# A recurrent attention layer fused with a maxout network: a new hand-written order of all engines and loads, grouped by matmul tile shape

## The chip, the cores and the metric

The kernel runs on one core of a Trainium2 chip. Time is device microseconds (us) of that core. PE is TensorE, the matrix engine; PEld is its weight load, which overlaps with matmuls; DVE is VectorE, ACT ScalarE, POOL GpSimd, and SP the engine that mostly issues DMAs. Each engine works through its own list of instructions in order and waits on semaphores for the others.

## What is computed

```python
def _attn_ref(q, k, v, alpha):                 # (4, 8, 768, 48) each
    state = np.zeros((B, H, D, D))
    for t in range(S):
        state = alpha[:, :, t, :, None] * state + np.einsum('bhd,bhe->bhde', k[:, :, t], v[:, :, t])
        y[:, :, t] = np.einsum('bhd,bhde->bhe', q[:, :, t], state)

def _moe_ref(x, w1, w2, w3, w_out):            # x: the y of all heads, (3072, 384); w1..w3 (384, 768)
    h = np.maximum(np.maximum(x @ w1, x @ w2), x @ w3)
    return h @ w_out
```

The state of each of 4 x 8 heads is a 48 x 48 matrix that decays by alpha and takes up one outer product per token; the 8 heads of a token, side by side, are the input of the maxout network.

## The kernel before

The 768 tokens of a batch are cut into chunks of 256 (W), so there are 12 steps: step s is chunk s // 4 of batch s % 4. Within a chunk two blocks (U) of 128 tokens are kept apart, and each partition holds a pair (R) of neighbouring tokens. A step loads alpha, q, k and v (384 KB each) into rings of four buffers, and computes the recurrence in its chunked form: sums of log alpha over the block by a matmul with a triangular matrix (`sums`, lines 234 to 242), exponentials of these sums (line 246), q and k scaled by them (line 266), scores of q against k (line 310), a mask (lines 316 and 320), then the product of masked scores and values together with the product of q and the state carried in (line 331), and the state's update (lines 389, 401, 405, 412). The first five steps turn q and k by TensorE transposes (line 289) and a copy; the later ones by transposing DMAs (line 296).

The network follows: `gate` (line 453) multiplies x by w2 - w1 and w3 - w1, `maxed` (lines 462 to 466) takes maxima with zero, and `project` (line 487) multiplies the result by w_out and x by w1 @ w_out, which the kernel computes itself at its start (lines 430 and 441). `scale_out` (lines 171, 173) moves the result out of PSUM, `store` writes it. The weights arrive in the same ring buffers as the steps' inputs (`load_weight`, line 120), in thirds of 384 KB.

Two sets name steps that are treated apart. A step in `BY_TOKEN` gets sums for each token: two triangular products for the second token of the pairs and two more for the first (lines 241, 242), and two exponentials of each sign. A step outside has them by pairs: alpha of both tokens is multiplied first (`pair_decay`, line 208), one sum is made, and the first token's k and q get the second token's alpha or its inverse by `near_k`, `near_q` and `inverse` (lines 222, 225, 217, 219). A step in `UNCOPIED` multiplies scores by values as they lie, in 64 matmuls of 64 rows (tile 64x32); one outside first copies the values of each block together (`unit_values`) and uses 32 matmuls of 128 rows (tile 128x32).

The order of all work is written out by hand in one string, `ORDER`. A word such as `G1@6#0` is: piece G (gate), its number 1, step 6, PSUM bank 0; a small letter at the end names the engine (v DVE, a ACT, p POOL; for loads and stores "a" is ACT's DMA queue, nothing is SP's). The letters that matter here: l load (0 alpha, 1 k, 2 q, 3 v), K weight load, m pair decay, N logarithms, r inverse, u near k, w near q, c sums, e and f exponentials, g totals, k and q scaling, V values scaled, v values copied, T and t transposes and their copy, D transposing DMA, A scores, a mask, Y output products, x copy of x, S, s, z, y the state's update, sum, decay and spreading, d weight differences, b, B, n, C, P, p the product of w1 and w_out, G and h gate and maxima, O, o, W projection, scaling, store. H is a filler: so many matmuls of 512 columns (line 506) on zeros, whose result nobody reads. The kernel emits the pieces in this order, and each engine gets its instructions in it; nothing else schedules them. PSUM has eight banks, and a piece that takes a bank waits until the one before it there has been read.

Of the kernel before, what the change touches and what calls it, by code (L numbers as in the profile page):

```python
# [23 lines left out]
def kernel(  # L24
# [109 lines left out]
    upto, pick = cp[:, :P], cp[:, P:P + 2 * U]
    ident = cp[:, P + 2 * U:2 * P + 2 * U]
    pmask = cp[:, 2 * P + 2 * U:3 * P + 2 * U]
    strict = cp[:, 3 * P + 2 * U:4 * P + 2 * U]
    rowmask = cp[:, 4 * P + 2 * U:].rearrange("p (r q) -> p r q", r=R)
# [380 lines left out]
    def emit(order):  # L519
# [8 lines left out]
        l0@0 N0a@0 N1a@0 H13@0#0 c0@0#0,1 l0@1 N0a@1 K0@0 l2@0 l1@0 K2@0 d1p@0 K1a@0 l3@0 d0p@0 N1a@1 c0@1#2,3
        f1a@0 K3@0 g0a@0 M0v@0 f0a@0 q0v@0 e1a@0 e0a@0 f0a@1 f1a@1 K4@0 g0a@1 l0@4 b0v@0 l0@2 k0v@0 H7@0#4
        T1@0#4 T0@0#5 B0@0#6 t0v@0 t1v@0 H3@0#7 A1@0#7,0 a2v@0 A0@0#1,5 a1v@0 a0v@0 a3v@0 l3a@1 V0a@0 S0@0#4,7  # L530
        l1@1 H4@0#5 Y0@0#5,1 b1v@0 B1@0#0 l2@1 s0a@0 z0p@0 n0a@0 e0a@1 y0v@0 d2v@0 l0@3 Y3@0 x1v@0 s1v@0 n1v@0
        K5@0 l1@2 x0a@0 H3@0#4 G2@0#4 l2@2 e1a@1 k0v@1 V0a@1 N1a@2 N0a@2 c0@2#6,3 K6@0 f1a@2 q0v@1 m0p@4 N0a@4
        S0@1#1,7 s0a@1 M0p@1 e1a@2 h2a@0 z0v@1 H2@0#0 T0@1#0 t0a@1 m0v@3 T1@1#5 f0a@2 t1v@1 H2@0#2 A1@1#2,1
        a2v@1 a3v@1 l0@5 K7a@0 y0p@1 e0a@2 N0a@3 g0a@2 c0@4#4 g0a@4 Y3@1#0 e0a@4 G0@0#5 f0a@4 d3p@0 l3@2 k0v@2
        K8@0 A0@1#2,1 a1v@1 c0@3#3 g0a@3 r0a@4 q0p@2 l2@3 a0v@1 G3@0#6 b2a@0 G1@0#4 M1v@0 K11@0 s1v@1 h3v@0 l3@4
        M0v@2 h0a@0 Y0@1#1 e0a@3 T0@2#2 x0v@1 r0a@3 m0p@5 d4p@0 x1a@1 l1a@4 B2@0#7 z1p@0 T1@2#6 G0@1#5 t0v@2
        N0a@5 c0@5#1 n2a@0 t1v@2 h1v@0 K9@0 K10@0 V0a@2 A0@2#0,2 a1v@2 a0v@2 h0a@1 g0a@5 G1@1#7 h1v@1 r1a@3
        d5p@0 l1@3 S0@2#6,4 G2@1#2 s0a@2 z0v@2 y0p@2 f0a@3 e0a@5 w0v@3 q0p@3 G4@1#0 A1@2#5,7 a2v@2 l0@6 G5@1#6
        G4@0#3 h4a@1 C2a@0 f0a@5 r1a@4 l3@3 V0a@4 v1a@4 Y3@2#5 a3v@2 Y0@2#0 x0v@2 x1v@2 u0p@4 l0@8 h2v@1 s1v@2
        G3@1#1 h3v@1 G5@0#7 h4a@0 h5v@0 G2@2#0 l2@4 u0v@3 G4@2#5 G5@2#2 k0p@4 S0@4#4,1 s0v@4 G1@2#3 l0@7 r0a@5  # L540
        l2@5 C0a@0 C1a@0 k0v@3 M0p@4 M1p@1 z0p@4 m0v@6 h2a@2 h4a@2 r0a@6 r1a@5 h5v@1 P0@0#7 p0a@0 G0@2#4 h0v@2
        l1@5 y1p@0 T1@3#0 l1@6 l3@6 t1v@3 T0@3#5 l3@5 l3@8 N0a@6 c0@6#6 v0p@4 P1@0#7 V0a@3 S0@3#4,0 h5v@2 z1v@1
        P2@0#2 m0p@8 v0p@3 w0p@4 s0v@3 h1v@2 t0a@3 p1a@0 M0v@3 z0p@3 p2v@0 s1v@4 G3@2#4 A1@3#3,5 a2v@3 a3v@3
        g0a@6 l2@6 q0v@4 f0a@6 y1a@1 u0v@5 m0p@7 l0@9 v1a@3 M1p@2 z1p@2 y0a@3 l3@7 l2@7 N0a@8 O0@1#7 A0@3#2,1
        M0p@6 O1@0#3 o0a@1 N0a@7 e0a@6 a1v@3 a0v@3 k0p@5 T1@4#5 t1v@4 u0p@6 k0p@6 o1a@0 r0a@7 l1a@7 V0a@6 T0@4#7
        s1v@3 h3v@2 t0v@4 c0@8#6 g0a@8 e0a@8 O1@1#1 o1a@1 Y0@3#2 w0v@5 q0p@5 x0a@3 c0@7#5 Y2@3#3 A0@4#0,4 a0v@4
        a1v@4 Y3@3 A1@4#7,1 a2v@4 V0a@5 a3v@4 e0a@7 x1a@3 r1a@6 O0@0#2 o0v@0 S0@6#0,4 G2@3#7 D1@5 D0@5 s0v@6
        y0p@4 g0a@7 M0v@7 w0p@6 q0p@6 D1@6 D0@6 G5@3#1 G0@3#3 h2v@3 v0v@6 G4@3#2 Y0@4#0 r0a@8 V0a@8 r1a@8 f0a@8
        f0a@7 h4a@3 y1a@2 Y1@4 Y3@4#7 Y2@4 x1v@4 x0v@4 O0@2#6 G1@3#5 M0v@5 u0v@7 z0p@6 G3@3#2 o0v@2 h5v@3 s1v@6
        k0p@7 M1p@4 V0a@7 v0a@7 S0@5#7,0 s0v@5 h3v@3 h0a@3 h1v@3 l0a@10 G2@4#6 A0@5#1,4 h2a@4 G0@4#7 r1a@7  # L550
        G4@4#2 h4a@4 W0@0 v0a@5 r0a@9 G5@4#3 a1v@5 a0v@5 r1a@9 z0p@5 y0a@5 M1p@3 G1@4#5 v1p@5 m0p@9 w0p@7 s1v@5
        h0v@4 l2@10 l1@10 A1@5#6,2 a2v@5 a3v@5 h1v@4 G3@4#4 Y1@5#1 W0@1 W1@0 l0@11 A1@6#0,7 a3v@6 l1@8 l2a@8
        a2v@6 O1@2#6 A0@6#2,5 a1v@6 l3a@11 r0a@10 o1a@2 m0p@10 N0a@10 q0p@7 a0v@6 N0a@9 z1v@4 Y3@5#7 Y2@5 x1a@5
        Y0@5 O0@3#0 c0@10#5 v1v@6 h5v@4 W0@2 W1@1 z1p@3 S0@7#6,2 s0v@7 D1@7 x0a@5 G1@5#7 v1v@8 G0@5#3 h3v@4
        G4@5#6 Y0@6#1 z0p@7 h0v@5 s1v@7 h4v@5 y0a@6 g0a@10 M1p@6 z1p@6 D0@7 r1a@10 m0p@11 l1@9 w0v@8 h1v@5 y1a@3
        G2@5#4 c0@9#3 Y1@6 l3a@10 x0a@6 Y3@6#2 Y2@6 u0p@8 w0p@10 k0p@8 M0p@10 q0p@8 D0@8 G5@5#6 N0a@11 h2a@5
        O1@3#7 f0a@9 o1v@3 h5v@5 x1a@6 y0a@7 G2@6#1 o0a@3 O1@4#4 h2v@6 A0@7#7,6 a0v@7 e0a@10 y1a@6 a1v@7 g0a@9
        l2a@9 e0a@9 u0p@10 D1@8 c0@11#2 u0p@9 e0a@11 f0a@11 o1a@4 S0@8#0 O0@4#1 V0a@10 f0a@10 M0p@8 v1p@7 s0v@8
        G3@5#7 h3v@5 z0p@8 o0a@4 g0a@11 M1v@7 z1p@7 A1@7#6,3 a3v@7 G0@6#4 h0a@6 q0p@10 l3a@9 W1@3 W0@3 W0@4
        l2a@11 k0p@10 r0a@11 G3@6#5 h3v@6 a2v@7 G1@6#0 Y1@7#7 G4@6#1 h4a@6 A0@8#2,3 a1v@8 A1@8#4,5 Y3@7#6 Y2@7  # L560
        x1a@7 M1p@5 z1p@5 D1@10 D0@10 W1@2 a3v@8 Y0@7 G5@6#1 x0v@7 O1@5#3 a0v@8 y0a@8 G2@7#6 Y3@8#5 G4@7#7 a2v@8
        h1v@6 G0@7#2 o1a@5 h0v@7 W1@5 S0@10#4 h4a@7 V0a@9 O0@5#0 o0a@5 h5v@6 k0p@9 w0p@9 s0v@10 z0v@10 Y2@8
        h2v@7 A1@10#3,2 q0v@9 G5@7#7 h5v@7 D1@9 D0@9 l1@11 O1@6#0 x1a@8 v0a@10 o1a@6 r1a@11 v0p@8 y1p@4 y0p@10
        Y0@8#1 A0@10#4,6 Y1@8 x0v@8 S0@9#7 G1@7#5 G2@8#0 h2a@8 O0@6#1 v1p@10 M0p@9 a2v@10 s0v@9 h1v@7 a3v@10
        w0v@11 G3@8#0 a1v@10 a0v@10 G4@8#3 h3v@8 G3@7#7 G5@8#5 h3v@7 u0p@11 k0p@11 M0p@11 W0@5 o0a@6 v0a@9
        V0a@11 v1p@11 Y0@10#2 G1@8#6 q0p@11 Y1@10 W1@6 x0a@10 Y3@10#4 Y2@10 A1@9#0,7 a2v@9 x1v@10 a3v@9 G0@8#1
        O0@7#2 W1@4 o0v@7 h0a@8 h1v@8 G1@10#0 S0@11#4 G2@10#7 h4v@8 h2a@10 z0p@9 y0a@9 y1a@5 A0@9#2,1 a0v@9
        G0@10#6 h0v@10 G3@10#3 W0@6 G5@10#7 O1@7#2 h1v@10 G4@10#6 s0v@11 z0v@11 y0a@11 Y3@9#0 h5v@8 h3v@10
        O1@8#4 h4a@10 D1@11 D0@11 a1v@9 o1v@7 W1@7 y1p@7 Y1@11#5 o1v@8 v1a@9 Y1@9#3 Y0@9 Y2@9 A0@11#6,1 a0v@11
        x0a@9 O0@8#2 x1v@9 G0@9#4 h0a@9 A1@11#6,3 G2@9#0 v0v@11 o0a@8 h5v@10 O1@10#4 a1v@11 a2v@11 O0@10#2  # L570
        Y3@11#7 o0a@10 h2v@9 a3v@11 Y2@11 Y0@11 x0v@11 G5@9#1 G1@9#6 x1a@11 G0@11#2 G4@9#0 G3@9#3 h1v@9 h0a@11
        G4@11#5 h3v@9 h4a@9 h5v@9 G2@11#7 h2a@11 G3@11#6 W0@8 W0@10 o1v@10 W1@8 W1@10 O0@9#2 G1@11#3 h1v@11
# [39 lines left out]
```

## Time and profile before

| | |
|---|---|
| median of 3 runs | 152.28 us (151.87 to 152.46) |
| profiled execution | 151.54 us |
| span of the profile, first to last instruction | 149.8 us |
| mean granted clock of TensorE | 0.984 |
| DMA | 32.53 MB in 73032 packets |
| PE, DVE, ACT, POOL busy | 138.3, 108.3, 89.6, 83.2 us |
| gate matmuls, L453 | 432, 54.1 us busy |
| projection matmuls, L487 | 225, 43.4 us busy |
| fillers, L506 | 34, 10.8 us busy |

An engine's busy time is the time in which at least one of its instructions runs. Matmuls are pipelined: one of 256 columns shows 273 ns, while the next starts 109 ns after it. So the pitch, start to start, is what a matmul costs, and not its own length. "x16" behind a line of the chain or timeline says how many instructions were merged.

### The profile page before, as it was taken

Reading aid. Unit: us, or ns where it says so; the run is one execution under the profiler, and the core shown is the slowest. Engines: PE = TensorE matmul, PEld = TensorE weight load, DVE = VectorE, ACT = ScalarE, POOL = GpSimd, SP = SyncE. Lnnn points to the kernel's source line nnn. Section 1 sums busy time; section 2 is a strip of 40 time slices with the busy share of each in tenths; the row PEclk is TensorE's granted clock in tenths of the full one; section 3 lists DMA queues with packets and bytes.
Section 4 is the critical chain, followed back from the end, with each engine's and each line's share of the span. In section 5 each row is a group of like instructions: output and inputs, shape, how many; then the busy total and the mean of one; then the engine's idle time right before and its main releaser. Section 6 shows DMA issues by size and latency. Waiting matters only on the chain.

```text
span 149.8 us, 5459 instructions
## 1 busy us (share of the span) xinstructions
PE 138.3 (92%) x2312; PEld 96.5 (64%) x2312; DVE 108.3 (72%) x206; ACT 89.6 (60%) x191; POOL 83.2 (56%) x109
## 2 busy tenths in 40 slices
PE   6977959879999999999999989999999999999990
...
GB/s 111 334 348 338 290 257 265 352 307 345 356 245 296 278 278 308 310 172 221 336 281 340 200 207 123 264 241 142 128 250 86 23 121 53 38 84 44 105 105 105
DMA packets 73032, 32.53 MB, mean 217 GB/s; under 512 B 65456, under 2 KB 73008, under 8 KB 73008
## 3 DMA queue, kind: packets, MB, share of 16 engines
...
q14 instruction: 6, 0.05, 0.1%
...
## 4 chain that ended last, share of the span: by engine, by line
PE 52%; DMA 15%; DVE 14%; ACT 6%; SPq 6%; issue 3%; POOL 2%; DVEq 0%
PE bank L453 22%; PE bank L487 18%; DMA wst<-in_moe_w_out_dram 5%; DMA qkT<-qk 5%; PE bank L331 5%; SPq L120 4%; PE bank L310 4%; DMA rq<-in_q_dram 3%; DVE lat L320 3%; DVE qk L266 2%; DMA rk<-in_k_dram 2%; SPq L104 2%; PE bank L389 2%; DVE lat L316 2%; ACT wo L165 1%
## 5 line engine op out<-in xcount | busy, mean ns | idle before, releaser
L453 PE MATMUL bank<-xT,wdif 128*128 128x256 f16 x432 | 54.1, 273 | 1.9 <-issue 0.7
L453 PEld LDWEIGHTS <-wdif 128*128 128x128 f16 x432 | 40.1, 98 | 10.3 <-issue 1.7
L462 DVE TENSOR_TENSOR hT<-bank,h 128x512 f16<-128x512 f32 x36 | 24.3, 685 | 6.8 <-PE bank L453 6.4
L320 DVE TENSOR_TENSOR lat<-bank,cp 128x512 f16<-128x512 f32 x36 | 23.4, 682 | 5.7 <-PE bank L310 5.7
L487 PE MATMUL bank<-wo,hT 128*128 128x384 f16 (+1 forms) x150 | 27.5, 320 | 0.0
L466 ACT ACTIVATE h<-bank 128x512 f16<-128x512 f32 x24 | 14.0, 594 | 17.2 <-PE bank L453 13.8
L487 PEld LDWEIGHTS <-hT 128*128 128x128 f16 x150 | 14.5, 98 | 8.9
L171 ACT ACTIVATE ob<-bank,c 128x384 f32<-128x384 f32 (+1 forms) x15 | 8.5, 572 | 15.3 <-PE bank L487 14.2
L266 POOL TENSOR_TENSOR qk<-rk,ic 128x768 f16<-128x768 f32 x8 | 14.5, 1818 | 2.6 <-PE bank L487 1.8
L487 PE MATMUL bank<-w1o,xT 128*128 128x384 f16 (+1 forms) x75 | 15.9, 321 | 0.0
L266 POOL TENSOR_TENSOR qk<-rq,ac 128x768 f16<-128x768 f32 x8 | 14.8, 1849 | 1.3 <-DMA rq<-in_q_dram 0.5
L171 ACT ACTIVATE vt<-rv,c 128x768 f16<-128x768 f32 x12 | 11.2, 936 | 3.7 <-DMA rv<-in_v_dram 3.6
L506 PE MATMUL bank<-hT 128*128 128x512 f16 x34 | 10.8, 459 | 1.3 <-DVE hT L579 1.2
L310 PE MATMUL bank<-qkT 48*64 48x128 f16 x384 | 9.7, 221 | 1.4 <-DMA qkT<-qk 0.6
L212 ACT ACTIVATE la<-ra 128x384 f16<-128x384 f32 x15 | 7.5, 522 | 5.3 <-DMA ra<-in_alpha_dram 5.2
L310 PEld LDWEIGHTS <-qkT 48*64 48x64 f16 x384 | 6.4, 106 | 5.9 <-issue 3.2
L222 POOL TENSOR_TENSOR rk<-rk,ra 128x384 f32<-128x384 f32 x6 | 6.2, 1040 | 6.7 <-DMA rk<-in_k_dram 6.7
L165 ACT CAST xT<-bank 128x384 f16<-128x384 f32 x13 | 6.1, 478 | 6.3 <-PE bank L331 6.3
L464 DVE TENSOR_SCALAR h<-bank 128x512 f16<-128x512 f32 x12 | 8.2, 682 | 2.0 <-PE bank L453 2.0
L208 POOL TENSOR_TENSOR ra<-ra 128x384 f32<-128x384 f32 x7 | 7.0, 999 | 4.6 <-DMA ra<-in_alpha_dram 4.4
L167 DVE CAST xT<-bank 128x384 f16<-128x384 f32 x11 | 5.9, 552 | 4.9 <-PE bank L331 4.8
L173 DVE TENSOR_SCALAR ob<-bank,c 128x384 f32<-128x384 f32 (+1 forms) x10 | 5.8, 593 | 4.8 <-PE bank L487 4.3
...
## 6 DMA issues: line engine op xcount, KB each, us to landing
...
```

The source lines that it names most:

```text
L165: nc.scalar.copy(out=dst, in_=src)
L171: nc.scalar.mul(dst, src, col)
L212: nc.scalar.activation(out=la, in_=raw("a", s, r), func=AFT.Ln, scale=float(np.exp(R * LAM)) if r == 0 else 1.0)
L266: engines[eng].tensor_mul(dst, src, by)
L310: nc.tensor.matmul(aps[i][to * J:(to + 1) * J, a * U + n, :], qkT[rows, r, 1, p, cols], qkT[rows, :, 0, p, cols], start=True, stop=True)
L320: nc.vector.tensor_mul(lats[s % 2][u][:, i], bank(("aps", s, u, i), [HP, P]), pmask.unsqueeze(1).broadcast_to([P, HP, P]))
L453: nc.tensor.matmul(gps[:, j, :], wdif[:, f, g, jj * P:(jj + 1) * P], xT[:, f].rearrange("p u t -> p (u t)"), start=(f == 0), stop=(f == NF ...
L462: nc.vector.tensor_max(hTs[s % NH][:, 2 * jg:2 * jg + 2, :], gps, h)
L464: nc.vector.tensor_scalar_max(h, gps, 0.0)
L466: nc.scalar.activation(out=h, in_=gps, func=AFT.Relu)
L487: nc.tensor.matmul(ops, lhs, (w1o if what == "x" else wo16)[:, j, cols], start=((what, j) == every[0]), stop=((what, j) == every[-1]))
L506: nc.tensor.matmul(wps, blank[:, :P], blank, start=True, stop=True)
```

## The change

The order is a new one from the first word to the last, with other banks, other choices of engine and other places of loads, stores and fillers. Steps 1 and 2 leave `BY_TOKEN` and `UNCOPIED`, so that only step 0 stays in them. The constants are split in two loads: `ca` (triangles, block selectors and the three column constants, 68 KB) on ACT's queue at once, and `cb` (identity and masks, 131 KB) as a piece of its own, J, on SP's queue. Step 1 now starts ahead of step 0, and the first load is a third of w1.

```diff
-    BY_TOKEN = (0, 1, 2)
-    UNCOPIED = (0, 1, 2)
+    BY_TOKEN = (0,)
+    UNCOPIED = (0,)
...
-    cp_np = np.concatenate(
-        [upto_np, pick_np.reshape(P, -1), np.eye(P, dtype=np.float16), pmask_np, strict_np, rowmask_np], 1)
+    ca_np = np.concatenate([np.concatenate([upto_np, strict_np, pick_np.reshape(P, -1)], 1).view(np.float32), c32_np], 1)
+    cb_np = np.concatenate([np.eye(P, dtype=np.float16), pmask_np, rowmask_np], 1)
...
-    def load_const(*_):
-        nc.scalar.dma_start(cp, nc.inline_tensor(cp_np, name="cp").ap())
-        nc.scalar.dma_start(c32, nc.inline_tensor(c32_np, name="c32").ap())
-
-    load_const()
+    def load_const(_, i, eng):
+        c, c_np = ((ca, ca_np), (cb, cb_np))[i]
+        queues[eng].dma_start(c, nc.inline_tensor(c_np, name=f"c{i}").ap())
+
+    load_const(0, 0, "a")
...
-        "l": load_step, "K": load_weight, "H": warm,
+        "l": load_step, "J": lambda _, i, eng: load_const(0, 1, eng), "K": load_weight, "H": warm,
...
-        l0@0 N0a@0 N1a@0 H13@0#0 c0@0#0,1 l0@1 N0a@1 K0@0 l2@0 l1@0 K2@0 d1p@0 K1a@0 l3@0 d0p@0 N1a@1 c0@1#2,3
-        f1a@0 K3@0 g0a@0 M0v@0 f0a@0 q0v@0 e1a@0 e0a@0 f0a@1 f1a@1 K4@0 g0a@1 l0@4 b0v@0 l0@2 k0v@0 H7@0#4
-        T1@0#4 T0@0#5 B0@0#6 t0v@0 t1v@0 H3@0#7 A1@0#7,0 a2v@0 A0@0#1,5 a1v@0 a0v@0 a3v@0 l3a@1 V0a@0 S0@0#4,7
-        l1@1 H4@0#5 Y0@0#5,1 b1v@0 B1@0#0 l2@1 s0a@0 z0p@0 n0a@0 e0a@1 y0v@0 d2v@0 l0@3 Y3@0 x1v@0 s1v@0 n1v@0
-        K5@0 l1@2 x0a@0 H3@0#4 G2@0#4 l2@2 e1a@1 k0v@1 V0a@1 N1a@2 N0a@2 c0@2#6,3 K6@0 f1a@2 q0v@1 m0p@4 N0a@4
...
+        K0@0 J0@0 l0@1 b0v@0 H14@0#0 B0@0#0 r0a@1 m0v@1 N0a@1 H5@0#1 c0@1#1 n0v@0 r1a@1 l0@0 g0a@1 f0a@1 l2@1
+        w0v@1 N0a@0 e0a@1 N1a@0 H6@0#2 c0@0#2,3 f1a@0 g0a@0 f0a@0 q0v@1 e0a@0 l1@1 u0p@1 k0v@1 H4@0#4 T0@1#4
+        K1@0 d0v@0 K2@0 d1p@0 T1@1#5 t1v@1 t0a@1 H2@0#6 A0@1#6,7 l3@1 l2@0 e1a@0 a0v@1 V0a@1 v0a@1 v1a@1 a1v@1
+        l1@0 l3@0 S0@1#0,1 s0v@1 A1@1#3,5 a2v@1 k0v@0 q0p@0 H6@0#4 T1@0#4 T0@0#2 V0a@0 M0p@1 z0p@1 y0a@1 t1a@0
+        l0@2 r0a@2 m0p@2 a3v@1 S0@0#6,7 Y2@1#0 l0@4 m0p@4 t0v@0 s1v@1 K6@0 A1@0#3,4 a3v@0 s0a@0 M0p@0 z0p@0
+        N0a@2 A0@0#5,2 c0@2#1 K3@0 K4@0 d2p@0 K5@0 l1@2 u0p@2 l2@2 r1a@2 w0p@2 K8a@0 N0a@4 Y3@1 a2v@0 Y0@1#4
+        K7a@0 g0a@2 x0a@1 a1v@0 a0v@0 c0@4#6 M0p@2 d5p@0 e0a@2 x1v@1 H2@0#3 G1@1#3 G0@1#4 h0a@1 f0a@2 g0a@4
...
+        a1v@5 r0a@10 f0a@10 r1a@10 a3v@5 z0v@6 g0a@10 M0p@10 z1p@5 y0p@6 a2v@5 s1v@6 W0@0 O0@4#6 o0v@4 W0@2
+        e0a@10 O1@2#1 o1a@2 S0@7#3,2 A1@6#0,7 s0v@7 a2v@6 z0v@7 s1v@7 y0v@7 A0@6#4,6 a0v@6 l3@9 a3v@6 a1v@6 l1@9
...
+        G3@6#6 G2@7#1 G3@7#2 G1@7#4 l1@11 u0p@11 z1p@6 W1@4 k0v@8 h1v@6 D1@8 h3v@6 e0a@11 G0@7#5 h0a@7 h1v@7
+        h2a@7 h3v@7 G4@7#3 h4a@7 D0@8 G5@7#6 h5v@7 M1p@7 z1p@7 v0a@9 V0a@10 O0@6#0 A1@9#5,4 A0@9#1,2 a1v@9 a0v@9
+        S0@8#3 a2v@9 s0v@8 z0p@8 y0p@8 l3@11 a3v@9 o1v@5 k0p@11 O0@7#6 o0a@7 O1@7#2 o1v@7 r1a@11 v1a@8 D0@10
+        A0@8#1,5 a0v@8 A1@8#3,4 S0@10#7 a3v@8 a2v@8 a1v@8 O1@6#6 Y0@9#2 D1@10 l2@11 w0p@11 q0p@11 Y1@9 M0p@11
...
```

Pieces of one kind for two steps now often stand together (`S0@1#0,1` ahead of `A1@1`, `G2@7`, `G3@7`, `G1@7` in a row). What is counted in pieces stays as it is but for this: three scalings of values move from ACT to DVE, eight more value copies and four more inverses appear, four exponentials and two logarithms go, and fillers are 41 matmuls instead of 34.

More of the change, by code (lines that the diff above doesn't have):

```diff
@@ L124, in load_weight @@
                                   moe_w_out.rearrange("(j p) m -> p j m", p=P)[:, 2 * (i - 9):2 * (i - 8)])
-    cp = cpool.tile([P, 6 * P + 2 * U], FP16, name="cp")
-    c32 = cpool.tile([P, 3], FP32, name="c32")
-    def load_const(*_):
-        nc.scalar.dma_start(cp, nc.inline_tensor(cp_np, name="cp").ap())
-        nc.scalar.dma_start(c32, nc.inline_tensor(c32_np, name="c32").ap())
-    load_const()
[L134 to L138, printed above, removed]
+    ca = cpool.tile([P, P + U + 3], FP32, name="ca")
+    cb = cpool.tile([P, 4 * P], FP16, name="cb")
+    def load_const(_, i, eng):
+        c, c_np = ((ca, ca_np), (cb, cb_np))[i]
+        queues[eng].dma_start(c, nc.inline_tensor(c_np, name=f"c{i}").ap())
+    load_const(0, 0, "a")
+    half = ca.bitcast(FP16)
+    upto, strict, pick = half[:, :P], half[:, P:2 * P], half[:, 2 * P:2 * P + 2 * U]
+    c32 = ca[:, P + U:]
+    ident, pmask = cb[:, :P], cb[:, P:2 * P]
+    rowmask = cb[:, 2 * P:].rearrange("p (r q) -> p r q", r=R)
     vs_c, ys_c, undo_c = c32[:, 0:1], c32[:, 1:2], c32[:, 2:3]
@@ L527 @@
     ORDER = """
[L528 to L572, printed above, removed]
@@ L573 @@
-        h3v@11 O1@9#0 G5@11#1 O4@11#7,4 W0@7 o1v@9 W1@9 o0v@9 W0@9 O2@11#3 h4a@11 h5v@11 O5@11 O6@11 o2a@11
-        o1v@11 W1@11 O3@11 o0a@11 W2@11 W0@11
+        K0@0 J0@0 l0@1 b0v@0 H14@0#0 B0@0#0 r0a@1 m0v@1 N0a@1 H5@0#1 c0@1#1 n0v@0 r1a@1 l0@0 g0a@1 f0a@1 l2@1
+        w0v@1 N0a@0 e0a@1 N1a@0 H6@0#2 c0@0#2,3 f1a@0 g0a@0 f0a@0 q0v@1 e0a@0 l1@1 u0p@1 k0v@1 H4@0#4 T0@1#4
+        K1@0 d0v@0 K2@0 d1p@0 T1@1#5 t1v@1 t0a@1 H2@0#6 A0@1#6,7 l3@1 l2@0 e1a@0 a0v@1 V0a@1 v0a@1 v1a@1 a1v@1
+        l1@0 l3@0 S0@1#0,1 s0v@1 A1@1#3,5 a2v@1 k0v@0 q0p@0 H6@0#4 T1@0#4 T0@0#2 V0a@0 M0p@1 z0p@1 y0a@1 t1a@0
@@ new lines @@
+        l0@2 r0a@2 m0p@2 a3v@1 S0@0#6,7 Y2@1#0 l0@4 m0p@4 t0v@0 s1v@1 K6@0 A1@0#3,4 a3v@0 s0a@0 M0p@0 z0p@0
+        N0a@2 A0@0#5,2 c0@2#1 K3@0 K4@0 d2p@0 K5@0 l1@2 u0p@2 l2@2 r1a@2 w0p@2 K8a@0 N0a@4 Y3@1 a2v@0 Y0@1#4
+        K7a@0 g0a@2 x0a@1 a1v@0 a0v@0 c0@4#6 M0p@2 d5p@0 e0a@2 x1v@1 H2@0#3 G1@1#3 G0@1#4 h0a@1 f0a@2 g0a@4
+        M1p@0 d4p@0 s1v@0 y0v@0 b1v@0 d3v@0 Y0@0#2,5 x0v@0 Y3@0 x1v@0 G2@1#0 h2v@1 k0v@2 r0a@4 z1p@0 l3@2 l0@3
+        m0p@3 B1@0#4 G2@0#1 G0@0#7 l0a@5 e0a@4 r1a@4 h2a@0 h0a@0 b2a@0 K11a@0 l2@3 q0v@2 n1a@0 K10@0 h1v@1
@@ new lines @@
+        G3@1#2 G1@0#5 T0@2#0 h3v@1 T1@2#1 t1v@2 t0a@2 K9@0 G5@1#7 V0a@2 v1a@2 v0p@2 l0@6 m0p@6 B2@0#4 h1v@0
+        l1a@3 n2v@0 A1@2#3,2 a2v@2 a3v@2 A0@2#1,0 G4@0#5 a1v@2 a0v@2 G4@1#4 u0p@3 r0a@3 N0a@3 f0a@4 S0@2#3,2
+        s0a@2 H2@0#0 Y0@2#0 G3@0#1 l3@3 c0@3#6 z0v@2 y0v@2 h4a@1 h5v@1 l2@4 w0p@4 l1@4 u0p@4 r0a@5 x0a@2 Y2@2#3
+        Y3@2 x1a@2 m0v@5 h4a@0 f0a@3 e0a@3 r1a@3 G5@0#4 s1v@2 h3v@0 r1a@5 h5v@0 C1v@0 G5@2#7 G1@2#0 G0@2#3
+        G2@2#5 G4@2#2 w0v@3 g0a@3 N0a@5 C0a@0 c0@5#1 G3@2#4 C2v@0 q0v@3 l0@7 P0@0#6 h4a@2 h5v@2 h0a@2 g0a@5
@@ new lines @@
+        M1v@1 k0p@4 M0p@4 N0a@6 f0a@5 e0a@5 z1p@1 h2a@2 c0@6#2 g0a@6 f0a@6 k0v@3 e0a@6 h1v@2 V0v@3 M0v@3 v1p@3
+        P2@0#7 p2v@0 p0a@0 T1@3#3 t1a@3 T0@3#1 t0v@3 l2@5 P1@0#5 p1a@0 l1@5 u0p@5 k0p@5 h3v@2 S0@3#2,0 s0a@3
+        v0a@3 A0@3#7,6 A1@3#3,1 l3a@4 l0a@8 m0p@8 y1p@0 M0p@5 M1p@2 z1p@2 q0v@4 z0v@3 M0v@6 s1v@3 m0v@7 O1@1#5
+        o1a@1 a0v@3 a2v@3 l3@5 O0@0#4 w0v@5 a1v@3 N0a@7 c0@7#2 r0a@6 y0a@3 T1@4#0 t1v@4 l1@6 q0p@5 u0p@6 r0a@7
+        a3v@3 g0a@7 o0a@0 V0v@4 v1v@4 M1v@3 l3a@6 r1a@6 T0@4#5 f0a@7 e0a@7 t0a@4 v0v@4 O0@1#7 o0a@1 V0a@5 v0p@5
@@ new lines @@
+        k0p@6 O1@0#3 o1v@0 l0@9 S0@4#6,0 s0v@4 z0v@4 A1@4#1,4 a3v@4 a2v@4 A0@4#2,5 a1v@4 y0v@4 a0v@4 l2@6 s1v@4
+        w0p@6 y1p@2 q0p@6 Y2@3#7 Y3@3 r1a@7 Y0@3#3 x1a@3 x0a@3 l2a@7 O0@2#6 G2@3#4 h2v@3 G0@3#1 h0v@3 N0a@8
+        c0@8#5 g0a@8 D0@5 l0@10 m0p@10 S0@5#2,0 l1@7 u0p@7 k0p@7 r0a@8 r1a@8 y1a@1 v1v@5 m0v@9 N0a@9 Y2@4#7 Y3@4
+        e0a@8 D1@5 x1v@4 s0v@5 z0v@5 y0p@5 z1p@3 Y1@4#3 Y0@4 x0v@4 M1v@4 G4@3#4 G3@3#1 G1@3#7 h1v@3 G5@3#2 z1v@4
+        G4@4#3 c0@9#7 s1v@5 G5@4#0 w0v@7 h4a@3 h5v@3 G2@4#4 y1p@3 h4a@4 g0a@9 h5v@4 o0a@2 e0a@9 f0a@8 G0@4#2
```

24 lines of the change are left out of this document (added).

## The prediction

> **What bounds the kernel now.** I read the page first, then the engines by stretches, then the chain that ended last, then single stretches of the timeline.
>
> ```profile
> PE 138.3 (92%) x2312; PEld 96.5 (64%) x2312; DVE 108.3 (72%) x206; ACT 89.6 (60%) x191; POOL 83.2 (56%) x109
> ...
> PE   6977959879999999999999989999999999999990
> ...
> GB/s 111 334 348 338 290 257 265 352 307 345 356 245 296 278 278 308 310 172 221 336 281 340 200 207 123 264 241 142 128 250 86 23 121 53 38 84 44 105 105 105
> ```
>
> PE is full from the tenth slice on. The table by stretches (busy time of PE, PEld, DVE, ACT, POOL, then granted clock, DMA share, GB/s) shows who else is:
>
> ```profile
> 20.00:25.00 5.00, 4.08 (x60) 2.47 (x59) 2.27 (x3) 3.11 (x7) 1.38 (x4) 0.71 0.93 244
> ...
> 50.00:60.00 10.00, 10.00 (x174) 6.49 (x172) 10.00 (x16) 9.12 (x22) 8.75 (x10) 1.00 1.07 286
> 60.00:70.00 10.00, 9.83 (x198) 7.20 (x195) 9.96 (x21) 7.43 (x16) 7.82 (x9) 1.00 1.14 233
> ...
> 100.00:110.00 10.00, 10.00 (x164) 6.82 (x163) 7.27 (x14) 4.87 (x9) 4.43 (x10) 1.00 0.78 144
> ```
>
> Until about 35 us loads and the start's own chain rule; from 40 to 80 PE and DVE are both full (DVE 37.98 of 40 us); afterwards PE alone. The chain says the same: from 61.90 to 145.89 it is PE, matmul behind matmul, but for one wait of 7 us for a transposing DMA, of which PE itself stood only 0.7 us. Its pieces (start, length, what) show what PE time is made of:
>
> ```profile
> 105.79 0.34 PE bank L331 x16
> 106.12 0.35 PE bank L310 x16
> 106.47 0.28 PE bank L331 x12
> 106.75 0.36 PE bank L389 x16
> ...
> 112.95 0.76 PE bank L453 x6
> ...
> 133.35 5.35 PE bank L453 x48
> 138.69 1.46 PE bank L487 x9
> 140.16 0.66 PE bank L453 x6
> ```
>
> Six gate matmuls (L453, 128x128) cost 0.66 us behind others of their shape and 0.76 behind another shape; 48 in a row cost 5.35. Sixteen score matmuls (L310, 48x64) cost 0.35 alone, though two such pieces in a row cost 0.57 (95.07 us in the chain), so 0.22 is their work. **A change of tile shape costs PE 0.10 to 0.13 us**; I take 0.105, which makes the sum of all pieces agree with the full stretch.
>
> **PE's work, part by part.** Shapes are four: 128x128, 64x64 (L310 and L389), 128x32 and 64x32 (both L331). Counting neighbours of different shape in PE's instruction order gives 103 changes before and 48 after: 55 x 0.105 = 5.8 us. From where 150 gate and output matmuls are done (61.9 us before) it is 61 against 24: 3.9 us of it in the stretch where PE has no slack, 1.9 ahead of it.
>
> Steps 1 and 2 leave BY_TOKEN and UNCOPIED. This is one sum by token in the old start (start, length):
>
> ```profile
> 7.71 0.34 PE L237 MATMUL bank<-cp,la 128*128 128x4 f16 x8
> ...
> 7.92 0.32 PE L241 MATMUL bank<-la,cp 128*128 128x384 f16 x1
> ...
> 8.08 0.32 PE L242 MATMUL bank<-la,cp 128*128 128x384 f16 x1
> ```
>
> From starts: 0.21 for eight small ones, 0.16 for each wide one, so 2 x 0.16 + 0.21 + 2 x 0.16 = 0.85 against 0.16 + 0.10 = 0.26 by pairs, 0.59 saved. The uncopied product (64 matmuls, 0.65 us from 39.53 in the timeline, shape change taken off) becomes two pieces of 16 at 0.34 - 0.11: 0.2 saved. Two steps: 1.6 us. PE's list shrinks by 5.8 + 1.6 = **7.4 us**. Seven more filler matmuls (41 for 34, 0.21 each, 1.5 us) lie where PE waits anyway (20 us of PE's first 61.9 are waiting or filler); uncovered, they cost their 1.5.
>
> [...]
>
> **What the two steps add elsewhere.** ACT loses four exponentials (L246, 0.5 each) and two logarithms (0.52), gains four inverses (L217, L219, 0.52); the orders also move four pieces of ACT's state copying away: about 3 us less. POOL gets 86.1 us of listed work for 80.6 (four more near-key products at 1.04, four more value-copy pairs at 1.02, two near-query at 1.0; one difference, one key and one query product fewer at 1.8). DVE gets some 3 us more. ACT stays clear of PE; POOL and DVE are weighed next.
>
> **The start.** Slices of 3.745 us moved 0.42, 1.25, 1.30, 1.27 MB, so 1.67 by 7.5 us, 2.97 by 11.2, 4.24 by 15.0. The first loads were used when about 0.34 MB beyond their own sum had moved (query of step 0: own sum 1.77, used at 8.88 with 2.1). In the new order w1's first third, both constants and alpha of step 1 come first: own sum 0.99, so alpha 1 at 6.5, query at 8.75, key 9.9, K2 12.2, values 13.3, step 0's query 14.5 and key 15.8. Through L208 (0.71), L212 (0.5), the sum, L246, L225 (0.92), L222 on POOL (1.04), L266 (0.95) the first transposes run at 11.9, scores at 13.5; step 0's key is scaled at 17.1, its scores at 18.7, its four masks (0.68 each) end at 21.6, the copy of x at 22.2, and the first gate follows. Before, it stood at 18.85. But 6.5 us of PE's list are then done, and before, at 22.2, 6.6 were: level. The wait moves, the sum doesn't.
>
> **The middle.** From there to A0 of step 6 (61.6 us of PE's list left) DVE has 92 pieces (98 instructions): 35 masks and maxima at 0.60 start to start (1.28 us for two in the timeline, the last 0.68), 9 state sums at 0.27, 7 scalings and differences at 0.96, 6 decays at 0.43, and 35 others at 0.56 on average, 52.4 us in all. Before, from 21.6 to 74.0, the same length, DVE did 82 instructions with 5.1 us idle. At the 95% it reached from 40 to 80, A0 of step 6 starts at 21.6 + 55.2 = 76.8 and PE's end is 76.8 + 61.6 = 138.4; with the tail (eviction 0.58, store to the span's end, 3.9 after PE's last matmul as before) 142.3. PE's list alone gives 149.8 - 7.4 = 142.4. As the second keeps the old stalls and the first none behind 77 us, I add to the first the 1.6 us that PE stood after 61.9: **143.9, 5.9 less**. The 1.6 has bounds 0 and 5 (the old wait for step 7's transposes, 0.7 on PE out of 7.1 us waiting in the chain).
>
> A row speaks for a dearer middle, L225 on DVE before and after 62 us (count | busy, mean ns):
>
> ```profile
> L225 DVE TENSOR_TENSOR rq<-rq,ic 128x384 f32<-128x384 f32 x2 | 2.6, 1298 | 0.0
> ...
> L225 DVE TENSOR_TENSOR rq<-rq,ic 128x384 f32<-128x384 f32 x2 | 1.1, 548 | 0.0
> ```
>
> Twice as long while POOL is busy: up to 0.75 us on each DVE instruction that reads only SBUF. The new order has 58 of these for 43. At 0 to 0.5 us for each of the 15, that is 0 to 7.5; I take 0 beyond the means above, which hold some stretching already, and give the rest to a rival. [...]
>
> The profiled execution took 151.54 us with a span of 149.8; the median of the runs is 152.28. 152.28 - 5.9 = **146.4 us**.
>
> **Rivals.**
> 1. PE's list alone counts, and DVE keeps up: 7.4 to 9.5 less (the latter if the waits of the old front, 4.5 us between 22 and 62, are halved): 142.8 to 144.9. For it: 84 us without slack. Against: DVE's 92 pieces. Chance 0.25.
> 2. DVE becomes the bound of the middle through POOL: 4 of the 7.5 us are lost: 150.4. For: the rows of L225, POOL at 8.8 of 10. Against: most added ones are short copies. Chance 0.17.
> 3. Slower: POOL's chain to the last transposes. POOL ended step 11's query product at 118.2 with 79.2 us of listed work up to it, so 39 idle, much of it waiting for step 11's key (landed 112.10). The new list has 81.0 up to there. With the same idle it ends at 120.0; the transposes land 5.8 later (issues 2.6 in sum, 4.5 to landing), A0 of step 11 starts at 125.8 with 21.9 of PE's list left: 125.8 + 21.9 + 3.9 = 151.6 span, 1.8 more: 154.1. It decides once that piece starts after 124.0. Against: POOL and DMA are half idle from 100 to 120 us, and the key's load now stands ahead of four transposes. Chance 0.08.
> [...]
>
> **Numbers.** My forecast has 0.50 (own range 144.5 to 148.8). Half a per cent (0.76 us) is about what a measurement of this kernel tells from no change. Rival 2's upper part and 3's lower part give 0.05 within it; faster 0.87, slower 0.08. The range, 142.8 to 150.5, leaves out rival 3, the top of 2 and a little below 1.
>
> **What will show it.** Chain after some 60 us all PE with half the short pieces alone; L453 pieces mostly 0.66 apart; L241 and L242 once; DVE at 9.5 or more of 10 between 25 and 75; first L453 near 22 us; A0 of step 6 near 77 and of step 11 near 114 to 118. PE waiting on L296's transposes late, or L225, L405 and L208 on DVE at twice their length, would prove me wrong.

## The result and the profile after

The changed kernel takes 161.33 us (median of 4 runs, 160.33 to 162.81) where the old one, on the same chip, takes 152.37 (4 runs): a ratio of 1.058, 95% interval 1.050 to 1.065. It is slower by some 9 us; 146.4 had been forecast. The profiled execution took 161.03 us with a span of 159.2. A ratio compares only those runs of either kernel that lie within 1.5% of its fastest, on one chip, while a median holds all of them. The old kernel's own median is 150.44 to 152.48 us beside the different experiments below, so kernels are compared by ratios; a difference of two spans is rougher.

From the page: busy time, and PE by slices.

```profile
PE 134.7 (85%) x2241; PEld 98.7 (62%) x2241; DVE 121.6 (76%) x213; ACT 87.2 (55%) x182; POOL 91.9 (58%) x123
...
PE   7987758739994969949699989999889699999991
```

PE's busy time is less, as the shorter list wants, but the row of nines that began in the tenth slice now begins in about the twenty-first. DVE's busy time grew by 13.3 us for seven more instructions. The same four stretches as before, and the one from 70 to 80 us:

```profile
20.00:25.00 5.00, 3.46 (x84) 2.73 (x83) 4.19 (x9) 3.29 (x9) 2.82 (x5) 1.00 0.99 304
50.00:60.00 10.00, 6.88 (x110) 4.50 (x110) 9.97 (x17) 4.99 (x12) 6.53 (x7) 1.00 0.80 211
60.00:70.00 10.00, 9.04 (x173) 6.50 (x173) 9.77 (x20) 7.96 (x20) 8.11 (x11) 1.00 0.64 146
70.00:80.00 10.00, 6.93 (x123) 5.39 (x123) 9.81 (x16) 2.71 (x7) 9.30 (x12) 0.83 1.19 264
100.00:110.00 10.00, 10.00 (x168) 7.99 (x155) 7.50 (x12) 5.85 (x12) 9.84 (x8) 1.00 0.29 77
```

From 50 to 60 us DVE is as full as before, 9.97 of 10 us with 17 instructions, but PE, which had no gap there, is busy for 6.88 only: DVE fills its time and no longer keeps PE fed. From 100 to 110 PE is full again, as before. The chain of waits says the same (start, length, what):

```profile
48.34 1.34 DVE qk L266
...
55.30 1.34 DVE qk L266
56.64 1.88 DVE kept L405
...
68.75 1.88 DVE st L167
...
91.42 1.40 DVE st L167
...
126.85 6.82 PE bank L453 x61
...
140.52 7.21 PE bank L453 x66
```

L405 decays a state of 128x192 and L167 here copies half of it (64x192); undisturbed they take 0.35 and 0.25 us. The timeline of that place, DVE first, then POOL:

```profile
55.23 1.42 DVE L266 TENSOR_TENSOR qk<-rq,ac 128x768 f16<-128x768 f32 x1
56.57 1.96 DVE L405 TENSOR_TENSOR kept<-fa,gm 128x192 f32<-128x192 f32 x1
58.45 0.15 DVE L378 TENSOR_TENSOR gm<-ge 128x4 f32<-128x4 f32 x1
58.63 0.36 DVE L401 TENSOR_TENSOR fb<-bank,kept 128x192 f32<-128x192 f32 x1
58.90 0.55 DVE L208 TENSOR_TENSOR ra<-ra 128x384 f32<-128x384 f32 x1
...
75.19 1.24 DVE L208 TENSOR_TENSOR ra<-ra 128x384 f32<-128x384 f32 x1
```

```profile
54.83 1.00 POOL L222 TENSOR_TENSOR rk<-rk,ra 128x384 f32<-128x384 f32 x1
55.91 2.40 POOL L266 TENSOR_TENSOR qk<-rk,ic 128x768 f16<-128x768 f32 x1
...
75.00 1.01 POOL L222 TENSOR_TENSOR rk<-rk,ra 128x384 f32<-128x384 f32 x1
```

POOL's product of 2.40 us ends at 58.31; DVE's L405, started at 56.57, ends at 58.53, its own 0.35 us less 0.13 later. L208 on DVE takes 0.55 us at 58.90, where POOL does nothing, and 1.24 at 75.19: POOL's L222 ends at 76.01, and L208 0.42 later. It goes both ways: POOL's 2.40 for a product that takes 1.82 in the old kernel spans the end of DVE's L266 at 56.65.

I counted this for the whole trace: for each DVE instruction with all its operands in SBUF, its length less that of the same shape where POOL is idle (0.55 us for a product of 128x384, 0.95 for 128x768, 0.35 for L405, 0.25 for a copy of 64 partitions). Call the sum **standing**. Before it is 6.3 us over 43 instructions, after 16.6 us over 58. Of these 58, 22 stand for more than 0.15 us, and every one of the 22 ends its own length less some 0.13 us after the end of a POOL instruction. L320, the masks, which read PSUM, hold their time (44 instructions, 0.3 us too long in all). What in the chip makes the others wait no trace shows.

A ruler for the middle: from the transposes of step 2's query to A0 of step 6, PE's list (its pieces at their undisturbed pitch, shape changes included) is 42.0 us long, by an estimate from those pitches. The changed kernel takes 55.2 us for it, from 34.5 to 89.7. **13.2 us are lost there** by this estimate; against the quickest run of the same list below, 44.7 us, it is 10.5.

A small part of that is the clock: TensorE was granted 0.94 of it over this stretch (0.83 from 70 to 80 us, the row above). The kernel with POOL's products by token, below, had 1.00 there and still takes 54.0 us, with PE busy for 44.64 us of it instead of 46.85. So the clock explains some 1 to 2 us of the loss.

### The profile page after: what moved, and what is told of

It is laid out like the page before. It is cut to its first block, busy times and chain, and to the rows that moved or that the text cites. A ratio compares the mean times of both kernels' runs of the same rounds, so it can differ in the third digit from the quotient of the medians.

```text
span 159.2 us, 5339 instructions
## 1 busy us (share of the span) xinstructions
PE 134.7 (85%) x2241; PEld 98.7 (62%) x2241; DVE 121.6 (76%) x213; ACT 87.2 (55%) x182; POOL 91.9 (58%) x123
## 4 chain that ended last, share of the span: by engine, by line
PE 33%; DVE 33%; DMA 13%; SPq 7%; issue 7%; POOL 3%; ACT 1%; ACTq 0%; DVEq 0%; POOLq 0%
PE bank L453 16%; PE bank L487 11%; DVE lat L320 6%; DVE hT L462 4%; DVE qk L266 4%; DMA rq<-in_moe_w_dram 4%; SPq L120 3%; DMA rk<-in_moe_w_dram 3%; DVE st L167 3%; DMA qkT<-qk 3%; SPq L104 3%; PE bank L331 3%; DMA rk<-in_k_dram 3%; DVE kept L405 2%; DVE vu L167 2%
## 5 line engine op out<-in xcount | busy, mean ns | idle before, releaser
L453 PE MATMUL bank<-xT,wdif 128*128 128x256 f16 x432 | 51.9, 276 | 5.6 <-DVE xT L167 2.2
L320 DVE TENSOR_TENSOR lat<-bank,cb 128x512 f16<-128x512 f32 x44 | 28.3, 682 | 2.7 <-PE bank L310 2.6
L487 PE MATMUL bank<-wo,hT 128*128 128x384 f16 (+1 forms) x150 | 27.5, 320 | 0.0
L466 ACT ACTIVATE h<-bank 128x512 f16<-128x512 f32 x26 | 15.3, 598 | 19.0 <-PE bank L453 18.9
L487 PEld LDWEIGHTS <-hT 128*128 128x128 f16 x150 | 14.5, 98 | 8.9
L171 ACT ACTIVATE ob<-bank,ca 128x384 f32<-128x384 f32 (+1 forms) x17 | 9.3, 562 | 13.9 <-PE bank L487 11.6
L222 POOL TENSOR_TENSOR rk<-rk,ra 128x384 f32<-128x384 f32 x10 | 10.3, 1034 | 11.4 <-DMA rk<-in_k_dram 8.6
L487 PE MATMUL bank<-w1o,xT 128*128 128x384 f16 (+1 forms) x75 | 15.9, 321 | 0.0
L167 POOL COPY vu<-vt 64x384 f16<-64x384 f16 x22 | 11.7, 530 | 4.8 <-issue 3.2
L266 POOL TENSOR_TENSOR qk<-rk,ic 128x768 f16<-128x768 f32 x7 | 13.7, 1951 | 0.6
L506 PE MATMUL bank<-hT 128*128 128x512 f16 x41 | 12.8, 456 | 1.3 <-DVE hT L580 1.2
L225 POOL TENSOR_TENSOR rq<-rq,ic 128x384 f32<-128x384 f32 x7 | 7.3, 1043 | 11.4 <-DMA rq<-in_q_dram 9.1
L266 POOL TENSOR_TENSOR qk<-rq,ac 128x768 f16<-128x768 f32 x7 | 12.9, 1846 | 0.5
L208 POOL TENSOR_TENSOR ra<-ra 128x384 f32<-128x384 f32 x7 | 7.2, 1023 | 5.7 <-DMA ra<-in_alpha_dram 5.6
L217 ACT ACTIVATE ic<-ra 128x384 f32<-128x384 f32 x11 | 5.7, 522 | 8.3 <-DMA ra<-in_alpha_dram 4.4
L165 ACT CAST xT<-bank 128x384 f16<-128x384 f32 x15 | 6.8, 483 | 5.7 <-PE bank L331 5.6
L310 PE MATMUL bank<-qkT 48*64 48x128 f16 x384 | 8.2, 218 | 1.8 <-ACT qkT L165 0.9
L289 PE MATMUL bank<-cb,qk 128*128 128x128 f16 x80 | 6.3, 238 | 3.5 <-DVE qk L266 3.5
```

The lines of the kernel that those rows point to most:

```text
L167: engines[eng].tensor_copy(out=dst, in_=src)
L171: nc.scalar.mul(dst, src, col)
L222: engines[eng].tensor_mul(raw("k", s, 0), raw("k", s, 0), raw("a", s, 1))
L225: engines[eng].tensor_mul(raw("q", s, 0), raw("q", s, 0), decays["k"][s % 3][:, 0])
L266: engines[eng].tensor_mul(dst, src, by)
L310: nc.tensor.matmul(aps[i][to * J:(to + 1) * J, a * U + n, :], qkT[rows, r, 1, p, cols], qkT[rows, :, 0, p, cols], start=True, stop=True)
```

## The experiments

### Is it that DVE's pieces stand beside POOL?

**The wait by itself.** A kernel of its own, without the layer: eight of each kind of DVE instruction alone, then the same beside 80 POOL products of 128x768 in a row.

> Only a measurement; nothing of the layer is computed. Seven kinds of DVE instruction, eight in a row of each, first while POOL rests, then while POOL runs 80 products of 128x768 of about 1.8 us back to back. Theory A: kinds that work in SBUF alone (product of 384 columns 0.55, of 768 0.95, scaling 0.60, casting copy 0.25, f16 copy 0.25) last 1 to 2.5 us beside POOL, each ending one own length after the end of a POOL instruction; the two that read PSUM stay at 0.68 and 0.55. If contention were a shared bandwidth instead, all SBUF kinds would stretch by one factor below 2.

DVE's timeline (start, length of the group, what):

```profile
3.80 4.11 DVE L59 TENSOR_TENSOR prod<-src,other 128x384 f32<-128x384 f32 x7
...
20.75 2.25 DVE L65 CAST cst<-src 64x192 f16<-64x192 f32 x8
...
25.10 5.76 DVE L69 TENSOR_TENSOR psm<-bank,src 128x512 f16<-128x512 f32 x8
...
36.41 16.68 DVE L59 TENSOR_TENSOR prod<-src,other 128x384 f32<-128x384 f32 x8
...
89.42 15.00 DVE L65 CAST cst<-src 64x192 f16<-64x192 f32 x8
...
117.56 5.75 DVE L69 TENSOR_TENSOR psm<-bank,src 128x512 f16<-128x512 f32 x8
```

Beside POOL, whose product takes 1.90 us on average here (1.80 beside the casts, 2.40 beside DVE's products of 128x768, so it stands too), a DVE product of 128x384 takes 2.08 us (0.55 alone) and a cast of 64x192 1.88 (0.28 alone): one per POOL instruction, whatever its own length. Scaling (0.65 to 2.08) and the f16 copy (0.28 to 1.66), with one input each, do the same. With a bank of PSUM as an input nothing changes (0.72 us each for the product, 0.59 for the cast, with and without POOL).

**Less of POOL.** In the changed kernel, POOL's products, decays and copies of steps from 4 on are cut to one head (values from step 6); the same in the old kernel.

```diff
+    def cut(s, eng, n):
+        return 1 if eng == "p" and s >= 4 else n
...
-        engines[eng].tensor_mul(dst, src, by)
+        h = cut(s, eng, H)
+        engines[eng].tensor_mul(dst[:, :, :h], src[:, :, :h], by[:, :, :h])
```

> The new kernel with POOL's products and copies of steps 4 to 11 (value copies from step 6) cut to one head, an eighth or a quarter of their columns, in the same order; the rest of the columns is left unwritten. [...] Theory A (DVE stands behind POOL's running instruction): DVE's 16 us of waiting fall to 4 or less and the span goes from 159 to 146 to 151. Theory D (the order is out of step for other reasons: loads, ACT, the engines' lists waiting on one another): no better than 155.

> The old kernel with the same cut of POOL's pieces, as the base of the run before: DVE waits 6 us behind POOL there. Theory A: 147 to 149.5, so that new minus old shrinks from 9 us to about 0 or below. Theory D: the difference stays at 5 or more.

The cut leaves columns unwritten, so these two only show times. The new kernel takes 150.09 us (ratio to the old one 0.990, interval 0.979 to 1.000), the old one 151.86 with the cut (0.999, 0.994 to 1.005), where 147 to 149.5 had been expected: its standing falls from 6.3 to 2.8 us, and it gains nothing by that, as PE had hardly a gap. So POOL's length costs the old order nothing and the new one some 10 us by the ratios: its span falls from 159.2 to 147.6, DVE's standing to 5.1 us, and the middle takes 44.7 us, 2.7 over the list:

```profile
50.00:60.00 10.00, 10.00 (x218) 6.81 (x207) 9.67 (x23) 9.21 (x22) 3.78 (x11) 1.00 0.92 243
```

DVE is as busy as it was, with 23 instructions for 17. But this cut shortens POOL's own chain of results too; the two kernels with POOL's work in shorter instructions, further down, separate that.

**Less of DVE.** The same cut on DVE's side.

```diff
-        return 1 if eng == "p" and s >= 4 else n
+        return 1 if eng == "v" and s >= 4 else n
```

> The changed kernel with DVE's (not POOL's) products, state decays and copies that read only SBUF cut to one head for steps from 4 on (value copies from 6): 18 instructions, 9.7 us of own length, of which about 7 are left out, so the output is not the reference's. Theory (they stand for POOL's instruction whatever their own length): DVE's waiting stays at 11 to 17 us, and the end moves by 2 to 5 us, much less than the 11.6 us that the same cut on POOL's side gave. Rival (DVE simply has too much work of its own): the end moves by 7 us or more.

156.37 us, ratio 1.038 (1.029 to 1.046); span 154.6, 4.6 less than the changed kernel, and some 3 us less by the ratios. Standing, counted against the uncut lengths, is still 15.4 us, and short instructions stand like long ones (DVE, then POOL; L273, L386 and L414 here are L266, L378 and L405):

```profile
53.94 1.77 DVE L386 TENSOR_TENSOR gm<-ge 128x4 f32<-128x4 f32 x1
...
62.84 1.47 DVE L414 TENSOR_TENSOR kept<-fa,gm 128x48 f32<-128x48 f32 x1
```

```profile
53.71 1.98 POOL L273 TENSOR_TENSOR qk<-rk,ic 128x768 f16<-128x768 f32 x1
...
62.43 1.81 POOL L273 TENSOR_TENSOR qk<-rq,ac 128x768 f16<-128x768 f32 x1
```

A product of 128x4, 0.15 us of work, took 1.77. With some 7 us of DVE's own work left out the kernel gains 3, where the cut on POOL's side gained 10: DVE's own amount of work is the smaller part of what was lost.

**POOL's work in shorter instructions.** Nothing is left out: POOL's products of 128x768 go as two of 128x384; then as four of 128x192, with the 128x384 ones halved as well.

```diff
-        engines[eng].tensor_mul(dst, src, by)
+        if eng == "p":
+            for r in range(R):
+                engines[eng].tensor_mul(dst[:, r], src[:, r], by[:, r])
...
```

> The changed kernel with each 128x768 product of POOL (L266) issued as two of 128x384, nothing left out. POOL then has the same elements to do and a little more overhead (two at about 1.0 us for one at 1.82). Theory (a DVE instruction that reads only SBUF stands until POOL's running instruction ends): the longest waits, of up to 1.6 us beside L266, fall to at most 0.9; of DVE's 16.6 us of such waiting some 4 to 5 go, and of the span 1 to 4 us (changed kernel 159.2). Rival (the two engines share SBUF's rate, or POOL's own chain of results is what is late): waiting and span stay as they are or grow with POOL's added 0.2 us per product.

> The changed kernel with each of POOL's products L208, L222, L225 in two of 128x192 and L266 in four, nothing left out. At 0.5 us for one of 128x192 (L405's length on POOL) POOL's busy time stays near 92 us or grows by some 5. Theory: no DVE instruction waits more than about 0.6 us beside these; the 16.6 us of waiting fall to 7 to 9, and the span by 2 to 6 us. Rival (rate shared, or POOL's chain): waiting and span unchanged or longer.

By token: 158.95 us, ratio 1.052 (1.044 to 1.061), standing 14.4 us, the middle 54.0; too little to tell from the changed kernel, and the fall in standing is half of what was expected. By half a token: 156.01, ratio 1.032 (1.023 to 1.042), an interval wholly below the changed kernel's; the gain is some 4 us by the ratios. Standing is 10.5 us, more than the 7 to 9 expected, the middle takes 48.1 us at a granted clock of 1.00, as by token, and the span of the profiled execution, the fastest of four, is 152.8. This is though POOL has 11.3 us more to do, where 5 at most had been expected:

```profile
PE 134.7 (88%) x2241; PEld 98.6 (65%) x2241; DVE 115.1 (75%) x213; ACT 87.1 (57%) x182; POOL 103.2 (68%) x189
```

The same decay that took 1.96 us in the changed kernel, with the scaling ahead of it (L274 and L414 are L266 and L405):

```profile
51.04 1.00 DVE L274 TENSOR_TENSOR qk<-rq,ac 128x768 f16<-128x768 f32 x1
51.97 0.66 DVE L414 TENSOR_TENSOR kept<-fa,gm 128x192 f32<-128x192 f32 x1
```

The longest wait of a DVE instruction falls with POOL's instruction: 1.62 us beyond its own length in the changed kernel, beside products of 128x768 (1.8 us alone); 0.85 by token, beside 128x384 (1.0); 0.42 by half a token, beside 128x192 (0.6), but for one wait of 1.62 at 12.6 us behind a weight difference of 128x768 that is not split. All 27 instructions that stand for more than 0.15 us there again end about their own length less 0.13 us after a POOL instruction; there are more of them than the 22, so the sum falls less than the longest does.

POOL had more work and the kernel got faster, so the loss was not that POOL's results came late. They are next, though: the chain of waits by engine now has POOL at 22%, where the changed kernel has it at 3%.

```profile
PE 35%; POOL 22%; DVE 18%; DMA 10%; issue 7%; SPq 3%; ACT 3%; ACTq 1%; POOLq 0%; DVEq 0%
```

In these kernels and the changed one the middle's excess over its 42.0 us follows the standing of the whole run: 13.2 us with 16.6 us, 12.0 with 14.4, 6.1 with 10.5, 2.7 with 5.1, and 9.6 with 15.4 where DVE's own work is cut as well.

### What it is not

**The two steps out of the sets.** The old order, with steps 1 and 2 taken out of `BY_TOKEN` and `UNCOPIED` and the pieces that this needs put in: two pair decays, four inverses, two near-key and two near-query products, four pieces of value copies (two copies each) and two of output products; the change to the new order needs them too.

```diff
-    BY_TOKEN = (0, 1, 2)
-    UNCOPIED = (0, 1, 2)
+    BY_TOKEN = (0,)
+    UNCOPIED = (0,)
```

> The old order with steps 1 and 2 out of BY_TOKEN and UNCOPIED, nothing else moved: the second part of the change alone. PE does 1.6 us less; POOL gets five products and a pair of copies more, DVE two, ACT four inverses for four exponentials. Theory A: POOL's additions in the first 45 us cost DVE a little, 149 to 152. Were this part the cause of the slowdown, it would be 155 or more.

152.98 us, ratio 1.013 (1.005 to 1.020), standing 6.5 us. Alone it costs the old order 0.8 to 3.0 us by that interval, with hardly more standing; that is a third of the 9 us at most.

**The late query of step 2.** In the changed kernel PE waits 3.4 us at 34.5 us for the transposes of step 2's query, whose load was issued at 21.4, landed 11.0 us later and was used on POOL at 32.45. Here the loads of step 2's key and query go ahead of three loads of weights.

```diff
-K3@0 K4@0 d2p@0 K5@0 l1@2 u0p@2 l2@2 r1a@2 w0p@2 K8a@0
+l1@2 l2@2 K3@0 K4@0 u0p@2 r1a@2 w0p@2 d2p@0 K5@0 K8a@0
```

> The changed kernel with the loads of step 2's key and query moved on SP's queue ahead of w3's three loads (1.15 MB), and the difference that needs two of these moved behind step 2's near query on POOL. If the wait of 3.4 us at 34.5 us (transposes of step 2's query) is the query's late landing, it shrinks below 1.5 us and PE is some 2 us ahead at 40 us; if the waits of the middle are DVE's standing beside POOL, these stay, and the end moves by 0 to 2 us. Rival (the late start is what the kernel lost): the end moves by 3 us or more.

163.68 us, ratio 1.089 (1.079 to 1.099): slower than the changed kernel, where up to 2 us less had been expected, a miss. The wait went, and came back 3 us sooner at the gate that needs the weights, 4.0 us long (from the chain):

```profile
22.07 7.25 DMA ra<-in_moe_w_dram
...
29.45 1.81 POOL wdif L419
...
31.31 1.46 PE bank L453 x6
```

At the middle's start it is 2.9 us behind the changed kernel, and the middle takes 54.0 us. So the exchange only chose which load is waited for, and the middle's loss stays. In the runs that leave the loads as they are the query's wait came out at 1.2 us or less, so the 3.4 us are partly those of one execution.

**DVE's copies to ACT.** 13 copies and casts in the new order go from DVE to ACT.

```diff
-y0v@2
+y0a@2
...
-V0v@3
+V0a@3
```

> The new kernel with thirteen pieces moved from DVE to ACT, places in the order unchanged: state copies (y, 4), value scalings (V, 3), w_out casts (C, 2), value copies (v, 4). They read and write SBUF only and took DVE 13.9 us in the new kernel's trace, 7.3 at their shortest seen lengths. Theory A (a DVE instruction with all operands in SBUF stands until POOL's running instruction ends; DVE is the bound from 38 to 93 us): DVE loses the 13.9 us and PE follows, span 159 to 150 +- 3. Theory B (DVE simply has too many instructions): at most the 7.3 us count, 153 to 156. Theory C (loads come late in the new order, the query of step 2 first): 158 to 160.

160.82 us, ratio 1.059 (1.047 to 1.071): nothing gained, a miss. By the expectation this speaks for theory C, late loads, which the exchange of loads above did not bear out. DVE's busy time fell by 10.7 us and its standing to 11.7, but each copy now stands in ACT's list behind something else, and PE waits for ACT (3.2 us for L165, 3.0 for L171). It suggests that an engine's letter can't be changed without its place.

**Order and engines apart.** The new order with the old engine letters for 69 pieces, and the old order with the new letters.

```diff
-q0v@2
+q0p@2
...
-y0v@2
+y0p@2
```

> The new order with the old kernel's choice of engine for every piece that works in SBUF alone (69 of them change between DVE, POOL and ACT). Theory A: DVE's waiting behind POOL falls from 16 us towards the old 6, span 151 to 156. Theory C: the order itself is the cause, 158 to 161.

> The mirror: the old order with the new kernel's choice of engine for the same pieces. Theory A: the old kernel's DVE, full from 40 to 80 us, gets the waiting too, span 149.8 to 155 or more. Theory C: 149 to 152, no change worth speaking of.

200.04 us (ratio 1.323, 1.311 to 1.335) and 180.88 (1.194, 1.184 to 1.204). Both are far slower than either kernel, the first beyond all that was expected, the second within theory A's "155 or more"; their standing is 11.9 and 21.1 us. Order and letters belong together, and with so much of the loss elsewhere these two runs tell nothing of the cause.

### Are the shape changes worth what I charged?

The old kernel with 16 of PE's pieces from 40 us on moved next to others of their shape, engines and loads untouched: 76 shape changes for 103.

```diff
-A1@3#3,5 a2v@3 a3v@3 g0a@6
+A1@3#3,5 A0@3#2,1 a2v@3 a3v@3 g0a@6
...
-N0a@8 O0@1#7 A0@3#2,1 M0p@6
+N0a@8 O0@1#7 M0p@6
```

> The old kernel in which only PE's pieces are moved, sixteen pieces from 40 us on, by at most 4 us of PE's work, so that changes of tile shape go from 103 to 76; all other engines keep their lists. At 0.105 us each, 27 fewer are 2.8 us of PE. Theory 'a change costs PE 0.1 us, and the end is PE's': 149.8 to 147.0 to 148. [...]

The ratio is 0.981 (0.972 to 0.990), 3.0 us of 152.4, where 27 x 0.105 = 2.8 was expected; but only 2 of the 12 runs enter it. The medians, 151.37 of 12 runs and 152.48 of 23, differ by 1.1 us, and the ten others had granted clocks of 0.984 to 1.000, no lower than the old kernel's; so the gain is somewhere between 1 and 3 us. The price itself shows in PE's busy time from 40 us on, which fell from 104.84 to 102.36 us at a granted clock of 1.00 in both profiles, 2.5 us. The span of that execution hardly moved (149.6 against 149.8 us): PE waited instead, longest for ACT, 1.6 us. DVE's standing stayed at 6.3. Grouping by shape saves PE's work, and **this version is, by a little, the fastest here that computes everything**.

## Why the prediction was wrong

**The step that failed** is the middle: "At 0 to 0.5 us for each of the 15, that is 0 to 7.5; I take 0 beyond the means above, which hold some stretching already, and give the rest to a rival." The rows of L225, 1.30 against 0.55 us, had shown the very thing. Standing grew by 10.3 us over the whole run, more than the upper bound. Two errors made it small. I charged the 15 added instructions alone, while an instruction of either order stands or not by what POOL runs beside it; and I capped each at 0.5 us, below the 0.75 of that very row, where the cost is the rest of POOL's instruction, up to 1.6 us beside a product of 128x768. So the "52.4 us in all", at means that held the old order's collisions, was too short: from 23.2 us, the end of step 0's masks, to A0 of step 6 DVE was busy for 60.0 of 66.5 us. The 95% rate was not what failed; from 34.5 us on it was 97%, and the lengths were longer. A0 of step 6 was forecast at 76.8 and came at 89.7; with POOL cut it came at 77.5.

**Rival 2** named the cause, POOL, and priced it at 4 us lost; the span lost 15.3 against the forecast's 143.9. Of these, 12.9 had been lost by A0 of step 6 and 2.4 behind it: from there 63.2 us of PE's list and waits plus a tail of 3.9 were forecast, and 69.5 passed. "Most added ones are short copies" was the argument against it, and short copies stand as long as anything: a copy of 0.25 us took 1.88. The 2.4 us behind A0 of step 6 are not traced to one cause; the longest wait there, 1.3 us at 125.6, is one for which the profile names no releaser.

**PE's list** was right, as far as it can be read: where PE is hardly kept waiting (80 to 90, 100 to 110, 130 to 150 us) its pieces come at the pitch of that model, and in the old kernel regrouped PE's busy time fell by 2.5 us where 27 changes were priced at 2.8. The count of 48 changes takes L310, of 48 rows, and L389, of 64, for one shape; that was my assumption, which the old trace does not show. In the new order's trace the two stand side by side (from the chain, between 96 and 104 us):

```profile
98.97 0.30 PE bank L389 x12
99.27 0.03 PE bank L310
99.29 0.04 PE bank L389 x3
99.33 0.46 PE bank L310 x30
```

L310 and L389 alternate here without a gap of 0.1 us: all 46 matmuls of the four pieces take 0.83 us, the 0.30 of the first behind L487 included.

**The start** was nearly right: the masks of step 0 end at 23.2 (21.6 forecast) and the first gate starts at 23.8 (22). It did not stay level: about 4.5 us went between there and the transposes of step 2, 3.4 of them for the query, a wait that I had not placed.

**Rival 3**, POOL's chain to the last transposes, was not what counted: PE waited at most 1.6 us in all for transposing DMAs. A0 of step 11 started at 133.6, behind other matmuls and without a wait, with the 12.9 us of the middle in its start.

**What was to show it**: "L225, L405 and L208 on DVE at twice their length, would prove me wrong" did.
